# One core: a recurrent-memory attention and a GEGLU layer; shared weight pieces read back from a scratch, the remaining keys loaded by another engine, a copy moved to ACT

## The chip, the core and the metric

The kernel runs on one core of a Trainium2 chip. The metric is the device time of one execution in microseconds. Before the change it is 2309.16 us, the median of three runs (2306.65 to 2320.56).

## What is computed

The input `x` has 2048 rows of 1024. It goes through two layers, and a gate of each row mixes the results:

```python
g = sigmoid((x * gate_w).sum(-1, keepdims=True))
out = g * A(x) + (1 - g) * B(x)

def A(x):                       # 64 segments of 32 rows, one after the other
    mem = mem0                  # 8 rows
    for s in range(64):
        h = concat(mem, x[32*s : 32*s+32])          # 40 rows
        q, k, v = h @ Wq, h @ Wk, h @ Wv            # 32 heads of 128
        p = softmax(mask(q @ k.T * scale))          # memory rows are seen by all
        o = (p @ v) @ Wo
        mem, out_s = o[:8], o[8:]                   # the next segment needs mem

def B(x): return (gelu(x @ w_gate) * (x @ w_up)) @ w_down
```

Only `mem` passes from one segment to the next. Each of Wq, Wk, Wv and Wo has 8 MB, so that A needs 32 MB of weights in every segment.

## The kernel before

**Rows.** Of a segment's 32 rows of `x`, 24 go with the 8 memory rows into `hT`, a block of 32 columns that TensorE (PE) projects in the segment itself. The other 8 rows (the "rest" rows) depend on no memory. They are projected ahead, for four segments at a time, by extra runs of eight products ("fills", lines 839 to 850) that are put between the segment's own. `FILL` (line 883) says which one or two of six fills a segment holds: two for `s % 4` of 0 (k, then q) and 1 (v, then q), one for 2 (v) and 3 (k). Their q and k go to a buffer in HBM, `qk_scr`, and come back a segment at a time into the tile `qkr` (`load_qk`, line 540, 64 KB). `put_rest` (line 879) copies the 8 rest keys of every head out of `qkr` into columns 32 to 39 of `kT`, on GpSimd (POOL). The scores (line 703) read `kT`.

**Halves.** A segment does the heads in two halves, first `ua = s % 2`, then `ub = 1 - s % 2`. In the lists of steps r is 0 for the first half and 1 for the second. The order of a segment's products is written out: k, q and v of the first half (with the end of the last segment's output product between them), then k, q, the first half's output product, v, and the beginning of the second half's output product. `plan(s)` hangs everything else (evacuations, transposes, loads, stores) on points of this list: `on("o", 1, 0, f)` runs f just before piece 0 of the second output product. Each engine works its own instructions in this order.

**Weights.** A weight is cut into pieces of 128 x 2048 (512 KB, 4 KB in each partition), named (matrix, half, i), 64 pieces in all. 36 pieces have an SBUF slot of their own. The other 28 share 14 slots in pairs: pieces k 0 and 1, q 0 and 1, v 0 to 4, o 0, 1, 4, 5 and 6, of both halves. As the order of halves alternates, every shared slot is loaded once in each segment, 14 x 512 KB = 7.3 MB. `spent` (line 455) issues such a load on SyncE's (SP's) queue as soon as PE has used a slot. Neighbouring slots are loaded by one transfer when all of a group are spent; `GROUPS` (line 408) has k 0-1, q 0-1, v 0-1, v 2-3 and o 4-6.

Pieces of q, k and v come from the inputs, in rows of 4 KB. Wo's layout has rows of 1 KB, so in segments 1 to 10 `keep` (line 383) stores the ten shared o pieces into a scratch in HBM, one in a segment, at the point `("k", 0, 4)`. Later loads of o 4-6 come from `wg_scr` in rows of 12 KB, those of o 0 and o 1 from `wo_scr`, one by one, in rows of 4 KB.

**From one segment to the next.** The output product leaves two halves of its sum in different partitions of a PSUM bank. `fold(s, b)` (line 821) copies one of them to the tile `part` and adds the other to it (line 825), both on VectorE (DVE). `next_mem` (line 829) transposes the result on PE and puts the memory columns into the next `hT`.

**Waits.** A small planner (class `_Prog`) finds for every operation the earlier ones that wrote or read the same bytes, or used the same PSUM bank, and makes it wait for those of other engines. Tiles overlay each other: the stage tile `kS` (k before its transpose) and `pAB` (the probabilities) lie on `kT`; stage tiles `0S` and `1S` overlap `oRc`, which the store `o_scr<-oRc` (line 985) reads.

The 64 segments end at 1658 us. Then come the rest rows' output product and, from 1721 us on, the B layer's products, with their own weights; the change touches neither.

Of the kernel before, what the change touches and what calls it, by code (L numbers as in the profile page):

```python
# [210 lines left out]
def bass_gated_mix__memory_aug_recurrent_mem_tr__geglu_ffn__prompt_kernel(  # L211
# [34 lines left out]
    with ExitStack() as es:  # L246
# [16 lines left out]
        a_scr = nc.dram_tensor("a_scr", [NSEG, 4, SEG, 256], BF16)  # L263
        wo_scr = nc.dram_tensor("wo_scr", [16, 128, 2048], BF16)
        wg_scr = nc.dram_tensor("wg_scr", [2, 128, 3, 2048], BF16)

# [104 lines left out]
        def dst(t, k):  # L371
            return t[:, :].rearrange("p (h f) -> p h f", h=4) if k[0] == "o" else t[:, :]

        kept = set()
        wo_at = lambda k: wg_scr[k[1], :, k[2] - 4, :] if 4 <= k[2] < 4 + 3 else wo_scr[8 * k[1] + k[2]]

        def load_piece(t, k, lane):
            if k in kept:
                op("sp", lambda e: e.dma_start(t[:, :], wo_at(k)), rd=[("D", "wo", k)], wr=[t.r()], lane=lane)
            else:  # L380
                op("sp", lambda e: e.dma_start(dst(t, k), src(k)), wr=[t.r()], lane=lane)

        def keep(k):
            t = slots[home[k]]
            op("sp", lambda e: e.dma_start(wo_at(k), t[:, :]), rd=[t.r()], wr=[("D", "wo", k)], lane="wo")
            kept.add(k)
# [20 lines left out]

        GROUPS = {("k", 0): 2, ("q", 0): 2, ("v", 0): 2, ("v", 2): 2, ("o", 4): 3}
        lead = {(m, i + x): (m, i) for (m, i), n in GROUPS.items() for x in range(n)}
        for (m, i), n in GROUPS.items():  # L410
            assert all(home[m, 0, i + x] == home[m, 0, i] + x for x in range(n))
        held = {}
# [7 lines left out]
        def load_group(k0, n):  # L420
            m, u, i = k0
            h = home[k0]
            t, x = (wall, h - nkqv) if m == "o" else (sl, h)
            reg = ("S", slots[h].off, slots[h].off + n * PIECE)
            if m == "o":
                op("sp", lambda e: e.dma_start(t[:, x:x + n, :], wg_scr[u]), rd=[("D", "wo", (m, u, i + y)) for y in range(n)],
                   wr=[reg], lane=f"sl{h}")
            else:
                W = {"q": A_Wq, "k": A_Wk, "v": A_Wv}[m]
                v = W[i * 128:(i + n) * 128, 16 * u:16 * u + 16, :].rearrange("(y p) h e -> p y (h e)", y=n)  # L430
                op("sp", lambda e: e.dma_start(t[:, x:x + n, :], v), wr=[reg], lane=f"sl{h}")
# [243 lines left out]
        def turn(st, bank=TT):  # L675
            def f(e):
                for j in range(4):
                    ins = e.transpose(PBV[bank][:, j * 128:(j + 1) * 128], st[:, j * 128:(j + 1) * 128], ident[:, :])  # L678
                return ins
            op("pe", f, rd=[st.r(), ident.r()], wr=[BK(bank)])  # L680

        def trans(to, st, bank=TT):
            turn(stage[st], bank)
# [5 lines left out]
        b8 = lambda v, n: v.unsqueeze(2).to_broadcast([128, 8, n])  # L689

        def mask():
# [4 lines left out]
        def scores(u, masked=True):  # L696
# [3 lines left out]
            def f(e):  # L700
# [8 lines left out]
                return ins  # L709
            op("pe", f, rd=[qT.r(), qkr.r(256 * u, 256 * u + 128), kT.r()], wr=[BK(SS)])  # L710
            op("pool", lambda e: e.memset(pAB[:, 256:544].bitcast(FP32), 0.0), wr=[pAB.r(256)])
# [13 lines left out]
            def halves(k, w, after):  # L725
                return [op("dve", lambda e, c=c: e.transpose(tAB[:, c + 32 * k:c + 32 * k + 4 * w].rearrange("p (j x) -> p j x", j=4)[:, :, 0:32],  # L726
                                                             pAB[:, c:c + 256].rearrange("p (j k x) -> p j k x", j=4, k=2)[:, :, k, :]),
                           rd=[pAB.r(c, c + 256)], wr=[tAB.r(c, c + 256)], after=[x]) for c, x in zip((0, 256), after)]
            halves(0, 64, halves(1, 56, [fin, fin]))

# [90 lines left out]
        def fold(s, b):  # L821
            lo, hi = slice(64 * b, 64 * b + 64), slice(64 - 64 * b, 128 - 64 * b)
            pt, cs = part, slice(256 * b, 256 * b + 256)
            op("dve", lambda e: e.tensor_copy(pt[lo, :], PB[XO][hi, cs]), rd=[BK(XO)], wr=[pt.r()])  # L824
            return op("dve", lambda e: e.tensor_tensor(out=a_bf[lo, :], in0=PB[XO][lo, cs], in1=pt[lo, :], op=ALU.add),
               rd=[BK(XO), pt.r()], wr=[a_bf.r()])
# [51 lines left out]
        def put_rest():  # L878
            op("pool", lambda e: e.tensor_copy(kT[:, :, :, 32:40].rearrange("p j g c -> p (j g) c"),  # L879
                                               qkr[:, 1, :].rearrange("p (x c) -> p x c", c=8)),  # L880
               rd=[qkr.r(128, 256)], wr=[kT.r()])

# [11 lines left out]
        def fill0(m, r, b, st, G=0, h=hR):  # L894
            run(fill(m, r, b, h))
            fill_evac(m, r, G, b, st)
            fill_put(m, r, G, st)

        def plan(s):
# [8 lines left out]
            def on(m, r, n, *fs, s=s):  # L908
                at.setdefault((s, m, r, n), []).extend(fs)
# [19 lines left out]
            if not last and s == 0:  # L929
                on("k", 0, 4, lambda: load_h(s + 1))  # L930
            if 1 <= s <= 2 * len(PAIRS["o"]):
                on("k", 0, 4, lambda: keep(("o", s % 2, PAIRS["o"][(s - 1) // 2])))
# [243 lines left out]
```

## Time and profile before

| | us |
|---|---|
| median of three runs | 2309.16 |
| the profiled execution, whole | 2311.71 |
| its span, first to last instruction | 2309.9 |
| PE busy in the span | 2069.2 (90%) |
| DVE / ACT / POOL busy | 1044.2 / 541.9 / 423.4 |
| moved by DMA | 638.04 MB, of it 596.58 MB on SP's queue |
| granted PE clock, mean | 0.98 |

The profile page has a map of the span in 40 equal slices of 57.7 us. In it a digit is the busy share in tenths, for each engine and for the 16 DMA engines together. The view of waits names, for an engine, the instruction that waited, what ended the wait, the total, how often, and the longest. The view of windows gives the busy time of the engines in a stretch, and at the end of each row the granted PE clock, the busy share of the DMA engines and the GB/s. The timeline lists instructions with start, duration, engine, line, operation and tiles; a "q" behind an engine's name means that its sequencer issues a transfer. The trace also has a record of every DMA packet: queue, start, duration and size.

### The profile page before, as it was taken

Reading aid. Unit: us, or ns where it says so; the run is one execution under the profiler, and the core shown is the slowest. Engines: PE = TensorE matmul, PEld = TensorE weight load, DVE = VectorE, ACT = ScalarE, POOL = GpSimd, SP = SyncE. Lnnn points to the kernel's source line nnn. Section 1 sums busy time; section 2 is a strip of 40 time slices with the busy share of each in tenths; the row PEclk is TensorE's granted clock in tenths of the full one; section 3 lists DMA queues with packets and bytes.
Section 4 is the critical chain, followed back from the end, with each engine's and each line's share of the span. In section 5 each row is a group of like instructions: output and inputs, shape, how many; then the busy total and the mean of one; then the engine's idle time right before and its main releaser. Section 6 shows DMA issues by size and latency. Waiting matters only on the chain.

```text
span 2309.9 us, 69920 instructions
## 1 busy us (share of the span) xinstructions
PE 2069.2 (90%) x31393; PEld 982.4 (43%) x31393; DVE 1044.2 (45%) x2697; ACT 541.9 (23%) x1111; POOL 423.4 (18%) x819
## 2 busy tenths in 40 slices
PE   4588888989999899898998989988799999999999
PEld 2243443444444444444444444443464444444444
DVE  3344444454444544445444444454315446163462
ACT  1122222222222222222222222221113123032130
POOL 4422212222222221222222222221100000000000
PEclk9699999999999999999999999998999999999999
DMA  9989999999999999999999989998964440803520
GB/s 370 358 299 336 327 337 347 324 341 334 330 346 328 347 322 327 344 318 352 322 340 339 331 313 328 324 344 313 331 214 139 153 148 10 291 19 128 167 88 19
DMA packets 237563, 638.04 MB, mean 276 GB/s; under 512 B 22441, under 2 KB 91305, under 8 KB 230481
## 3 DMA queue, kind: packets, MB, share of 16 engines
q1 hardware_dynamic: 213440, 596.58, 72.9%
q0 software_dynamic: 13888, 26.31, 3.5%
q10 hardware_dynamic: 9936, 10.69, 1.3%
q8 instruction: 247, 4.05, 0.7%
q14 instruction: 52, 0.42, 0.1%
HBM read 596.85 MB, written 36.63 MB: 274 GB/s over the span
## 4 chain that ended last, share of the span: by engine, by line
PE 56%; DMA 32%; DVE 5%; issue 3%; ACT 2%; POOL 1%; SPq 0%; ACTq 0%; POOLq 0%; DVEq 0%
PE pb L780 18%; PE pb L1077 15%; DMA sl<-in_A_Wv_dram 10%; DMA wall<-wg_scr 7%; PE pb L1131 5%; DMA qkr<-qk_scr 3%; PE pb L813 3%; DMA o_scr<-oRc 3%; PE pb L796 3%; PE pb L678 3%; PE pb L850 3%; PE pb L1027 2%; PE pb L1112 2%; DMA sl<-in_A_Wq_dram 1%; DMA xr_scr<-xr 1%
## 5 line engine op out<-in xcount | busy, mean ns | idle before, releaser
L780 PE MATMUL pb<-sl,hT 128*32 128x512 bf16 x12288 | 776.1, 385 | 36.6 <-DMA sl<-in_A_Wv_dram 17.3
L780 PEld LDWEIGHTS pb<-sl,hT 128*32 128x32 bf16 x12288 | 312.5, 97 | 361.4 <-DMA sl<-in_A_Wv_dram 39.8
L850 PE MATMUL pb<-sl,hR 128*32 128x512 bf16 x3072 | 220.7, 392 | 3.5 <-issue 2.9
L1077 PE MATMUL pb<-xT,wg 128*128 128x512 bf16 x896 | 211.7, 379 | 0.8
L1077 PE MATMUL pb<-xT,wu 128*128 128x512 bf16 x896 | 211.7, 379 | 0.0
L813 PE MATMUL pb<-wall,oT 128*32 128x256 bf16 x4056 | 154.1, 278 | 33.7 <-DMA wall<-wg_scr 10.5
L824 DVE COPY part<-pb 64x256 f32<-64x256 f32 x128 | 54.0, 422 | 256.8 <-PE pb L813 256.0
L661 ACT ACTIVATE kS<-pb 128x512 bf16<-128x512 f32 x127 | 75.8, 597 | 385.1 <-PE pb L780 363.7
L796 PE MATMUL pb<-wall,oT 128*32 128x512 bf16 x2048 | 150.4, 389 | 9.8 <-issue 2.9
L763 POOL COPY oRc<-oT 128x128 bf16<-128x128 bf16 x128 | 96.3, 752 | 339.9 <-DVE oT L664 336.8
L1131 PE MATMUL pb<-wd,GT 128*128 128x512 bf16 x672 | 146.6, 379 | 2.7 <-DMA wd<-in_B_w_down_dram 2.6
L1085 ACT ACTIVATE s<-pb 128x512 f32<-128x512 f32 x112 | 66.8, 596 | 313.4 <-PE pb L1077 313.4
L813 PEld LDWEIGHTS pb<-wall,oT 128*32 128x32 bf16 x4056 | 96.9, 97 | 95.8 <-ACT oT L661 25.8
L714 ACT ACTIVATE E<-pb 128x320 bf16<-128x320 f32 x128 | 56.0, 437 | 333.8 <-DVE pb L713 333.8
L1086 DVE SCALAR_TENSOR_TENSOR tp<-s,pb 128x512 f32<-128x512 f32 x112 | 76.9, 687 | 125.9 <-ACT s L1085 125.7
L1077 PEld LDWEIGHTS pb<-xT,wg 128*128 128x128 bf16 x896 | 87.2, 98 | 107.9 <-DVE GT L1093 3.7
L1077 PEld LDWEIGHTS pb<-xT,wu 128*128 128x128 bf16 x896 | 87.7, 98 | 105.7
L879 POOL COPY kT<-qkr 128x128 bf16<-128x128 bf16 x128 | 37.3, 291 | 491.0 <-DVE kT L664 229.4
L664 DVE COPY kT<-pb 128x512 bf16<-128x512 bf16 x128 | 54.4, 425 | 160.9 <-PE pb L678 160.9
L664 DVE CAST oT<-pb 128x160 bf16<-128x160 f32 x256 | 76.5, 320 | 104.4 <-PE pb L746 104.4
L726 DVE STREAM_TRANSPOSE tAB<-pAB 128x128 bf16<-128x128 bf16 x512 | 114.0, 280 | 4.4
L1090 DVE SCALAR_TENSOR_TENSOR tp<-tp,pb 128x512 f32<-128x512 f32 x112 | 77.0, 687 | 78.5 <-ACT tp L1089 78.5
(103 smaller groups left out, 2158.6 us busy)
## 6 DMA issues: line engine op xcount, KB each, us to landing
sl<-in_A_Wv_dram SPq DMA_DIRECT2D x128, 1024.0 KB, 11.2
wall<-wg_scr SPq DMA_DIRECT2D x53, 1536.0 KB, 9.5
sl<-in_A_Wk_dram SPq DMA_DIRECT2D x64, 1024.0 KB, 6.1
sl<-in_A_Wq_dram SPq DMA_DIRECT2D x64, 1024.0 KB, 9.0
wall<-wo_scr SPq DMA_DIRECT2D x120, 512.0 KB, 6.2
wd<-in_B_w_down_dram SPq DMA_DIRECT2D x42, 1024.0 KB, 5.5
sl<-in_A_Wv_dram SPq DMA_DIRECT2D x75, 512.0 KB, 11.4
wall<-in_A_Wo_dram SPq DMA_DIRECT2D x41, 512.0 KB, 7.9
```

The costliest lines, as they stand in the source:

```text
L661: op("act", lambda e: e.activation(o, i, ACTF.Copy), rd=rd, wr=wr)
L664: op("dve", lambda e: e.tensor_copy(o, i), rd=rd, wr=wr, after=after)
L726: return [op("dve", lambda e, c=c: e.transpose(tAB[:, c + 32 * k:c + 32 * k + 4 * w].rearrange("p (j x) -> p j x", j=4)[:, :, 0:32], pAB[: ...
L763: op("pool", lambda e: e.tensor_copy(oRc[:, :, 16 * u:16 * u + 16].rearrange("p c x -> p x c"), oT[:, :, :, 32:40].rearrange("p g j c -> p ...
L780: ins = e.matmul(PB[bk][32 * g:32 * g + 32, :], lhsT=h[:, i, :], rhs=w[:, g * 512:(g + 1) * 512], start=(n == 0), stop=(n == 7))
L796: ins = e.matmul(PB[XO][32 * g:32 * g + 32, :], lhsT=oT[:, j, x, 0:32], rhs=wall[:, na:nb + 1:nb - na, c:c + 256], start=(n == 0 and hp == 0),
L813: ins = e.matmul(PB[XO][32 * g:32 * g + 32, 256 * b:256 * b + 256], lhsT=oT[:, j, x, 0:32], rhs=w[:, c:c + 256], start=False, stop=(n % 4 ...
L850: ins = e.matmul(PB[b][32 * g:32 * g + 32, :], lhsT=h[:, k[2], :], rhs=w[:, g * 512:(g + 1) * 512], start=(n == 0), stop=(n == 7))
L1077: ins = e.matmul(PB[bk][:, 0:FB], lhsT=w[:, kc, cc:cc + 128], rhs=xT[:, :, :, kc, :].rearrange("p t i c -> p (t i) c"), start=(kc == 0), s ...
L1086: op("dve", lambda e, hg=hg, t=t: e.scalar_tensor_tensor(out=t[:, :], in0=s1[:, :], scalar=1.0, in1=hg, op0=ALU.add, op1=ALU.mult), rd=[BK ...
L1090: op("dve", lambda e, hu=hu, t=t: e.scalar_tensor_tensor(out=t[:, :], in0=t[:, :], scalar=1.0, in1=hu, op0=ALU.add, op1=ALU.mult), rd=[BK( ...
L1131: ins = e.matmul(PB[bank[2 * k + hf]][:, :], lhsT=GT[:, j, tb * 128:(tb + 1) * 128], rhs=w[:, jj, hf * 512:(hf + 1) * 512], start=(j == 0) ...
```

## The change

There are four edits.

1. `put_rest` no longer counts as a writer of the whole `kT`. It writes a name of its own, `("K", "rest")`, which the scores read, and waits for the last readers of what lies on `kT` (the PE transposes of k and q, or the DVE transposes of `pAB`), collected in `turned`. The second `put_rest` of a segment is put ahead of the transposition of k.
2. The second load of rest queries and keys of a segment, `load_qk(s, 1)`, is issued by ACT instead of POOL.
3. The groups are now k 0-1, q 0-1, v 0-2, v 3-4, o 0-1 and o 4-6. Every group has a scratch in HBM with the pieces of a row side by side, so rows of 8 or 12 KB. The 18 shared pieces of v, k and q are stored into it in segments 3 to 20, one in each, in this order, at the point `("o", 1, 0)`. A group's transfer reads the scratch as soon as all its pieces are there, and the input before.
4. The first copy of the first `fold` of a segment is on ACT where `s % 4` is 0 or 3.

```diff
+        GROUPS = {("k", 0): 2, ("q", 0): 2, ("v", 0): 3, ("v", 3): 2, ("o", 0): 2, ("o", 4): 3}
+        run_scr = {g: nc.dram_tensor(f"{g[0]}{g[1]}_scr", [2, 128, n, 2048], BF16) for g, n in GROUPS.items()}
-        wo_at = lambda k: wg_scr[k[1], :, k[2] - 4, :] if 4 <= k[2] < 4 + 3 else wo_scr[8 * k[1] + k[2]]
+        def at_scr(k):
+            g = lead[k[0], k[2]]
+            return run_scr[g][k[1], :, k[2] - g[1], :]
...
-        GROUPS = {("k", 0): 2, ("q", 0): 2, ("v", 0): 2, ("v", 2): 2, ("o", 4): 3}
...
-            if m == "o":
-                op("sp", lambda e: e.dma_start(t[:, x:x + n, :], wg_scr[u]), rd=[("D", "wo", (m, u, i + y)) for y in range(n)],
-                   wr=[reg], lane=f"sl{h}")
+            ks = [(m, u, i + y) for y in range(n)]
+            if all(k in kept for k in ks):
+                op("sp", lambda e: e.dma_start(t[:, x:x + n, :], run_scr[m, i][u]), rd=[("D", "w", k) for k in ks], wr=[reg], lane=f"sl{h}")
...
-            op("pe", f, rd=[qT.r(), qkr.r(256 * u, 256 * u + 128), kT.r()], wr=[BK(SS)])
+            op("pe", f, rd=[qT.r(), qkr.r(256 * u, 256 * u + 128), kT.r(), ("K", "rest")], wr=[BK(SS)])
...
-            halves(0, 64, halves(1, 56, [fin, fin]))
+            turned[:] = halves(0, 64, halves(1, 56, [fin, fin]))
...
-            op("dve", lambda e: e.tensor_copy(pt[lo, :], PB[XO][hi, cs]), rd=[BK(XO)], wr=[pt.r()])
+            if b == 0 and s % 4 in (0, 3):
+                act_copy(pt[lo, :], PB[XO][hi, cs], [BK(XO)], [pt.r()])
+            else:
+                dve_copy(pt[lo, :], PB[XO][hi, cs], [BK(XO)], [pt.r()])
...
-               rd=[qkr.r(128, 256)], wr=[kT.r()])
+               rd=[qkr.r(128, 256)], wr=[("K", "rest")], after=turned)
...
+        STORE = [(m, i) for m in "vkq" for i in PAIRS[m]]
...
+            if 3 <= s < 3 + 2 * len(STORE):
+                on("o", 1, 0, lambda: keep((STORE[(s - 3) // 2][0], ub, STORE[(s - 3) // 2][1])))
...
-                on("v", 0, 5, lambda: load_qk(s, 1))
+                on("v", 0, 5, lambda: load_qk(s, 1, "act"))
...
+                on("o", 0, 0, lambda: put_rest())
                 on("o", 0, 0, lambda: trans(kT, ub, A0))
...
-                on("o", 0, 0, lambda: put_rest())
```

More of the change, by code (lines that the diff above doesn't have):

```diff
@@ L263, in bass_gated_mix__memory_aug_recurrent_mem_tr__geglu_ffn__prompt_kernel @@
         a_scr = nc.dram_tensor("a_scr", [NSEG, 4, SEG, 256], BF16)
-        wo_scr = nc.dram_tensor("wo_scr", [16, 128, 2048], BF16)
-        wg_scr = nc.dram_tensor("wg_scr", [2, 128, 3, 2048], BF16)
         PB = [es.enter_context(nc.psum_tensor(f"pb{i}", [128, 512], FP32)) for i in range(8)]
@@ L372, in dst @@
             return t[:, :].rearrange("p (h f) -> p h f", h=4) if k[0] == "o" else t[:, :]
+        GROUPS = {("k", 0): 2, ("q", 0): 2, ("v", 0): 3, ("v", 3): 2, ("o", 0): 2, ("o", 4): 3}
+        lead = {(m, i + x): (m, i) for (m, i), n in GROUPS.items() for x in range(n)}
+        for (m, i), n in GROUPS.items():
+            assert all(home[m, 0, i + x] == home[m, 0, i] + x for x in range(n))
+        run_scr = {g: nc.dram_tensor(f"{g[0]}{g[1]}_scr", [2, 128, n, 2048], BF16) for g, n in GROUPS.items()}
         kept = set()
-        wo_at = lambda k: wg_scr[k[1], :, k[2] - 4, :] if 4 <= k[2] < 4 + 3 else wo_scr[8 * k[1] + k[2]]
+        def at_scr(k):
+            g = lead[k[0], k[2]]
+            return run_scr[g][k[1], :, k[2] - g[1], :]
         def load_piece(t, k, lane):
             if k in kept:
-                op("sp", lambda e: e.dma_start(t[:, :], wo_at(k)), rd=[("D", "wo", k)], wr=[t.r()], lane=lane)
+                op("sp", lambda e: e.dma_start(t[:, :], at_scr(k)), rd=[("D", "w", k)], wr=[t.r()], lane=lane)
             else:
@@ L384, in keep @@
             t = slots[home[k]]
-            op("sp", lambda e: e.dma_start(wo_at(k), t[:, :]), rd=[t.r()], wr=[("D", "wo", k)], lane="wo")
+            op("sp", lambda e: e.dma_start(at_scr(k), t[:, :]), rd=[t.r()], wr=[("D", "w", k)], lane="wo")
             kept.add(k)
@@ L406, in first @@
                 fetch(n)
-        GROUPS = {("k", 0): 2, ("q", 0): 2, ("v", 0): 2, ("v", 2): 2, ("o", 4): 3}
-        lead = {(m, i + x): (m, i) for (m, i), n in GROUPS.items() for x in range(n)}
-        for (m, i), n in GROUPS.items():
-            assert all(home[m, 0, i + x] == home[m, 0, i] + x for x in range(n))
         held = {}
@@ L679, in f @@
                 return ins
-            op("pe", f, rd=[st.r(), ident.r()], wr=[BK(bank)])
+            return op("pe", f, rd=[st.r(), ident.r()], wr=[BK(bank)])
         def trans(to, st, bank=TT):
-            turn(stage[st], bank)
+            turned.append(turn(stage[st], bank))
             dve_copy(to[:, :, :, 0:32].rearrange("p j g c -> p (j g) c"),
@@ L689, in bass_gated_mix__memory_aug_recurrent_mem_tr__geglu_ffn__prompt_kernel @@
         b8 = lambda v, n: v.unsqueeze(2).to_broadcast([128, 8, n])
+        turned = []
         def mask():
```

## The prediction

> **What bounds the kernel now.** The page first: the profiled execution took 2311.71 us, 1.8 us more than its span, and 2.55 us more than the median of the runs. I sum against the profiled execution and take 2.5 off at the end.
>
> ```profile
> span 2309.9 us, 69920 instructions
> ...
> PE   4588888989999899898998989988799999999999
> ...
> DMA  9989999999999999999999989998964440803520
> ...
> q1 hardware_dynamic: 213440, 596.58, 72.9%
> ```
>
> In slices 3 to 28, the segments, PE and the DMA engines are both near full. Which one is late is told by PE's waits in 626 to 1585 us, the 40 segments in which all new groups are in use:
>
> ```profile
> PE pb L834 <- DVE a_bf L825: 21.9, 26, 1.1
> PE pb L703 <- POOL kT L879: 9.7, 11, 3.2
> PE pb L813 <- DMA wall<-wg_scr: 8.9, 13, 1.4
> PE pb L780 <- DMA sl<-in_A_Wv_dram: 6.0, 13, 0.7
> PE pb L813 <- DMA wall<-wo_scr: 5.5, 10, 1.2
> PE pb L780 <- DMA sl<-in_A_Wq_dram: 4.0, 4, 1.7
> ```
>
> Weights cost 24.4 us in 40 waits, rest keys 9.7 us. The view counts from a matmul's modelled end and so too little: at 1026.22 it tells 0.70 us, but the starts are 1.08 us apart, where groups of four follow in 0.21. With 0.17 us more for each wait the weights cost 31 us, 0.8 us of a segment's 24. The fold's 21.9 us is a chain DVE, PE, DVE.
>
> SP's queue and some windows show why weights are late although the engines rest in every segment:
>
> ```profile
> 998.38 0.32 SPq L426 DMA_DIRECT2D wall<-wg_scr  x1
> 998.74 1.38 SPq L540 DMA_DIRECT2D qkr<-qk_scr  x1
> 1005.16 0.32 SPq L985 DMA_DIRECT2D o_scr<-oRc  x1
> 1008.41 0.38 SPq L431 DMA_DIRECT2D sl<-in_A_Wk_dram  x1
> 1009.27 0.70 SPq L431 DMA_DIRECT2D sl<-in_A_Wq_dram  x1
> 1011.47 1.08 SPq L431 DMA_DIRECT2D sl<-in_A_Wv_dram  x2
> 1014.69 0.34 SPq L381 DMA_DIRECT2D sl<-in_A_Wv_dram  x1
> ```
>
> ```profile
> 1005.00:1009.50 4.50, 4.27 (x90) 2.31 (x92) 1.44 (x4) 0.10 (x1) 1.16 (x3) 1.00 0.47 153
> 1009.60:1013.20 3.60, 3.60 (x74) 1.68 (x66) 1.45 (x4) 0.43 (x2) 1.30 (x2) 1.00 0.95 274
> 1020.00:1022.50 2.50, 2.40 (x60) 1.14 (x61) 1.44 (x5) 0.99 (x3) 0.50 (x2) 1.00 1.03 416
> ```
>
> The last but one number is the DMA engines' busy share. A segment's stream starts with k, when PE has used its slots, and ends with o 4-6 some 24 us later, as long as the segment. Between streams lies a lull: in 1005.0 to 1009.5 a share of 0.47, so 4.5 x 0.53 = 2.4 us of all engines. So a shorter stream takes waits away, and a transfer added in the lull may be free.
>
> **Scratch rows.** In the packet records a 4096-byte packet takes 159 ns (median; mean 183), an 8192-byte one 309 (another queue), a 12288-byte one 460 (mean 486). Clean times save 2 x 159 - 309 = 9 ns on 8 KB and 3 x 159 - 460 = 17 on 12 KB. A group of two has 128 packets of 8 KB, 8 on each engine: k, q, v 3-4 and o 0-1 save 4 x 8 x 9 = 0.29 us, v 0-2 saves 8 x 17 = 0.14, together 0.43 us a segment: the low end. By means v 0-2 saves 8 x (3 x 183 - 486) = 0.5 us; k's megabyte takes 3.57 us of engine time, q's 2.97, a later v group's 2.59, and if all pairs came down to 8 x (309 + 26) = 2.68 us, the stream would save 1.6 us: the high end. I take 1.2, nearer to the second, since means are what the stream lives on. Against a mean loss of 0.8 us this takes most waits away: four fifths of 31, **-25 us**. In 342 to 626 us (segments 9 to 20, v in use by stages) weights cost 7.4 us in 9 waits; half of it with the same correction, **-4**.
>
> **Grouping.** PE uses v 3 just before v 4; now both land with v 4, which is the late one, and o 0 with o 1. One more group of four matmuls (0.21 us) waits until the stream has become faster, some ten segments: **+2**.
>
> **Eighteen stores.** The ten stores of o stand in the middle of the stream. The two last, where one o piece at most comes from Wo, had segments of 25.60 and 25.35 us (from one fold's transpose to the next), the next 23.49 and 23.81: 1.5 us or more each, so at most 27 us for 18. The new stores are issued behind o 4-6 and run into the lull: nothing at the low end. But three things queue behind. SP's load of rest keys is needed 5 us later, so is covered. `o_scr<-oRc` lands later, and ACT's evacuation to 0S or 1S waits for it (54.2 and 48.3 us of waits, 4.0 and 1.0 us of them on PE). And the next k group overwrites the slot being stored: its issue at 1008.41, and all SP work behind it, must await a store that cannot end before o 4-6, landed at 1008.77. That holds in four segments for k and in four for q. I take 0.4 us for the ten v stores and 1 us for the eight others: **+12** (0 to 27).
>
> **Rest keys.**
>
> ```profile
> 1014.84 0.29 POOL L879 COPY kT<-qkr 128x128 bf16<-128x128 bf16 x1 [1.76 <-DVE kT L664]
> 1015.43 0.55 POOL L540 DMA_DIRECT2D qkr<-qk_scr  x1 [0.29 <-POOL kT L879]
> 1021.62 0.29 POOL L879 COPY kT<-qkr 128x128 bf16<-128x128 bf16 x1 [5.37 <-DMA qkr<-qk_scr]
> ```
>
> The first copy no longer waits for DVE's copy of kT (0.42 us and its hop), and ACT, free until the exponential 2.4 us later, issues without the 0.29 us that POOL loses: the load starts some 0.75 us earlier. Behind the waiting ACT stand only that exponential and its followers. But POOL's 64 KB go as 16 packets of 4 KB, one an engine (landing 6.0 us after issue), ACT's as 128 of 512 bytes, eight an engine. The nearest rows of ACT's queue under load are the x stores of the beginning: issued at 62.82, first packet at 66.0, last at 68.0, landed at 68.85. There 512-byte packets and SP's alternate (half microseconds from 62.5: 18, 41, 38 against 40, 44, 46). Eight turns beside 8 or 12 KB are 8 x (27 + 309) to 8 x (27 + 486) ns, 2.7 to 4.1 us; with 3.2 before and 0.9 behind 6.8 to 8.2, so the landing is up to 1.4 us later than today. If ACT's start were SP's of an idle stream (1.2 us) it would be 2 us earlier. Today's waits are 12.7 us from 342 on. I take half of them gone, **-6** (-13 to +50).
>
> The Trainium skill ("DMA: Bandwidth & Descriptors", section on queues, rings and completion order) says that an engine drains a whole packet of some 9 to 17 descriptors from one ring before it switches. The alternating counts above do not agree with it; what it would give is the fourth rival.
>
> **Fold.** In segments with s % 4 of 0 and 3 DVE's copy starts 161 ns after the product, else 48: the fill's copy is ahead of it. ACT takes 303 ns for 160 columns and 437 for 320, so some 384 for 256 against 426. 32 x 0.13 = 4 us at best, half of it on the path: **-2**. At worst the extra hop (about 0.05 us) costs +2.
>
> **Sum:** -25 - 4 + 2 + 12 - 6 - 2 = -23, so 2288.7 for the profiled execution and **2286** for the median. One per cent, 23 us, is about what a measurement of this kernel can tell from no change.
>
> **Rivals.**
> - *The rows bring little* (0.25): only the clean 0.43 us, so half of the 31 and nothing before (-15), stores at 20, the rest as above: -15 + 2 + 20 - 3 - 2 = +2, 2311. For it: the late part of the stream already runs at 416 GB/s, and 12 KB rows at about the same. Against it: the 274 GB/s of its beginning.
> - *All waits go and the stores hide* (0.13): -31 - 9 - 13 - 4 = -57, 2252. For it: 2.4 us of lull against 1.5 us a store.
> - *The rest keys become the late transfer* (0.13): eight small packets queue between 12 KB ones, and PE stands before the scores. At the full 1.4 us, in some 40 segments, +50 in place of -6: +33, 2340. It ends slower than before from about 0.6 us a segment. For it: today the copy follows the landing within 0.12 us in most segments, so there is no slack. Against it: the earlier issue.
> - *The rest keys pass in one turn* (0.05): eight rows of 27 ns are 0.2 us, the landing comes 3.2 + 0.2 + 0.9 = 4.3 us after an issue that is 0.75 us earlier, and all 12.7 us go: -30, 2279. Against it: the counts.
>
> **How the numbers follow.** The forecast has 0.44, and runs from 2265 to 2302 by its own terms; two thirds of it lie over 1% faster. Faster by over 1%: 0.29 + 0.13 + 0.05 and a little of the first rival, 0.48. Slower by over 1%: 0.13 and its worst stores, 0.14. The range 2254 to 2325 leaves out the third rival and the tip of the second.
>
> **What would show it.** Right: the weights' waits on PE fall from 24.4 us to a few; k's transfer, landing 6.1 us after issue, lands in about 5; segments from 21 on take 23.2 us instead of 24; POOL's wait for rest keys shrinks. Wrong: the new transfers take as long as before; the wait before L703 grows; SP stands before the k group in segments 14 to 20.

## The result, and the profile after

The changed kernel takes 2345.34 us in the median of four runs (2343.91 to 2354.52), beside 2309.16 for the kernel before, which a fourth run leaves as it is. The ratio is 1.0168, with a 95% interval of 1.0143 to 1.0193: 1.7% longer, clear of the spread of the runs, if short of 2%. The forecast was 2286 in a range of 2254 to 2325; what came is 5 us from the third rival, 2340, "the rest keys become the late transfer".

Lines are numbered anew. The projections are at L784 (L780 before), the output products at L817 and L800 (L813, L796), the scores at L707 (L703), the fold's transpose at L841 (L834), the transposition of q and k at L680 (L678), `put_rest` at L886 (L879), `load_qk` at L542 (L540). Loads from a scratch are issued at L429, from the inputs at L433, stores of pieces at L391. The profile cannot tell a scratch's name apart in `wall<-o_scr`: it stands for o 0-1 as well as o 4-6. The page of the changed kernel, the same rows as before:

```profile
span 2344.2 us, 69748 instructions
...
PE   3588888878889898898989889898799999999999
...
DMA  9999999989988888898898888988865350713520
...
q1 hardware_dynamic: 174384, 606.02, 70.6%
```

The weights' larger rows did what rows can do: SP's queue moves 9.4 MB more (596.58 MB before, and the stores are in it) in 39,000 packets fewer, and its share of engine time falls from 72.9% to 70.6%. In 626 to 1585 us the DMA engines' share falls from 0.93 to 0.88, and PE's row has lost nines as well: both rest more. So the time was not lost to the stream's length. The waits of PE in 626 to 1585 us, the window of the prediction, say where it went:

```profile
PE pb L707 <- POOL kT L886: 56.3, 39, 2.1
PE pb L841 <- DVE a_bf L832: 19.2, 20, 1.0
PE pb L784 <- DVE hT L844: 5.3, 20, 0.3
PE pb L680 <- ACT 0S L663: 5.2, 3, 2.0
PE pb L817 <- DMA wall<-o_scr: 2.2, 4, 1.0
PE pb L680 <- ACT 1S L663: 2.1, 5, 0.7
```

Weights cost 2.2 us where they cost 24.4. The scores' wait for rest keys has risen from 9.7 us in 11 waits to 56.3 in 39, one in nearly every segment. The timeline of POOL and ACT in a segment, the same one (36) whose rows the prediction showed of before:

```profile
1046.25 0.30 POOL L886 COPY kT<-qkr 128x128 bf16<-128x128 bf16 x1 [1.27 <-PE pb L680]
1046.58 0.35 ACTq L542 DMA_DIRECT2D qkr<-qk_scr  x1
1055.29 0.29 POOL L886 COPY kT<-qkr 128x128 bf16<-128x128 bf16 x1 [7.17 <-DMA qkr<-qk_scr]
```

The first copy waits for PE's transpose and no longer for DVE, and the issue follows it after 0.03 us, as forecast. But the second copy now starts 8.71 us after the issue; before it was 6.19 (1015.43 to 1021.62). The transfers by their queue in the window 650 to 1600 us (kind, count, KB, median us from issue to landing):

```profile
sl<-k_scr SPq DMA_DIRECT2D x40, 1024.0 KB, 5.2
sl<-q_scr SPq DMA_DIRECT2D x39, 1024.0 KB, 7.7
qkr<-qk_scr ACTq DMA_DIRECT2D x39, 64.0 KB, 8.5
```

Before, in the same window:

```profile
sl<-in_A_Wk_dram SPq DMA_DIRECT2D x39, 1024.0 KB, 6.1
qkr<-qk_scr POOLq DMA_DIRECT2D x40, 64.0 KB, 6.2
```

and q landed 9.1 us after issue. So the big transfers became faster by 0.9 and 1.4 us and the small one slower by 2.3. The chain that ended last is now led by it, with nearly a fifth of the span:

```profile
DMA qkr<-qk_scr 18%; PE pb L784 16%; PE pb L1088 14%; PE pb L1142 5%; PE pb L817 4%; DMA o_scr<-oRc 3%; PE pb L857 3%; PE pb L1038 2%; PE pb L800 2%; DMA wall<-o_scr 2%; DMA sl<-in_A_Wv_dram 2%; PE pb L1123 2%; PE pb L680 2%; POOL kT L886 1%; DMA xr_scr<-xr 1%
```

**Early and steady.** Taking the start of the first fold's copy into `hT` as the beginning of a segment, folds 0 to 20 cover the segments in which pieces are stored, folds 20 to 60 the 40 segments after. In the profiled executions (2311.71 and 2346.1 us) the early part takes 496.5 us before and 525.9 after, the steady part 963.1 and 971.4. So 29 of the 34 us were lost *early*, where the wait for rest keys is small (13.9 us, before 4.0). The rest keys explain the steady part only. These two parts are given for every kernel below. They are of one execution each: kernels that run the same instructions in the steady part differ there by up to 14 us, so the verdicts rest on the medians and ratios, and the parts only say where.

### The profile page after: what moved, and what is told of

Read it like the earlier page. It is cut to its first block, busy times and chain, and to the rows that moved or that the text cites. A ratio compares the mean times of both kernels' runs of the same rounds, so it can differ in the third digit from the quotient of the medians.

```text
span 2344.2 us, 69748 instructions
## 1 busy us (share of the span) xinstructions
PE 2064.8 (88%) x31368; PEld 997.1 (43%) x31393; DVE 1031.0 (44%) x2665; ACT 554.0 (24%) x1143; POOL 389.7 (17%) x756
## 3 DMA queue, kind: packets, MB, share of 16 engines
q1 hardware_dynamic: 174384, 606.02, 70.6%
## 4 chain that ended last, share of the span: by engine, by line
PE 55%; DMA 33%; DVE 4%; ACT 3%; issue 2%; POOL 2%; ACTq 0%; POOLq 0%; SPq 0%
DMA qkr<-qk_scr 18%; PE pb L784 16%; PE pb L1088 14%; PE pb L1142 5%; PE pb L817 4%; DMA o_scr<-oRc 3%; PE pb L857 3%; PE pb L1038 2%; PE pb L800 2%; DMA wall<-o_scr 2%; DMA sl<-in_A_Wv_dram 2%; PE pb L1123 2%; PE pb L680 2%; POOL kT L886 1%; DMA xr_scr<-xr 1%
## 5 line engine op out<-in xcount | busy, mean ns | idle before, releaser
L784 PE MATMUL pb<-sl,hT 128*32 128x512 bf16 x12288 | 772.9, 387 | 25.8 <-DVE hT L844 8.8
L784 PEld LDWEIGHTS pb<-sl,hT 128*32 128x32 bf16 x12288 | 316.2, 98 | 336.6 <-issue 32.7
L817 PE MATMUL pb<-wall,oT 128*32 128x256 bf16 x4056 | 148.8, 278 | 19.9 <-DMA wall<-o_scr 7.5
L800 PE MATMUL pb<-wall,oT 128*32 128x512 bf16 x2048 | 150.5, 392 | 5.8
L666 DVE COPY part<-pb 64x256 f32<-64x256 f32 x96 | 40.4, 421 | 227.6 <-PE pb L817 227.6
L817 PEld LDWEIGHTS pb<-wall,oT 128*32 128x32 bf16 x4056 | 99.1, 98 | 74.1 <-ACT oT L663 26.7
L886 POOL COPY kT<-qkr 128x128 bf16<-128x128 bf16 x128 | 37.6, 294 | 549.2 <-DMA qkr<-qk_scr 398.6
L716 DVE TENSOR_REDUCE st<-pb 128x8 f32<-128x320 f32 x128 | 62.9, 492 | 135.0 <-PE pb L710 135.0
```

What stands on the lines that cost most here:

```text
L666: op("dve", lambda e: e.tensor_copy(o, i), rd=rd, wr=wr, after=after)
L784: ins = e.matmul(PB[bk][32 * g:32 * g + 32, :], lhsT=h[:, i, :], rhs=w[:, g * 512:(g + 1) * 512], start=(n == 0), stop=(n == 7))
L800: ins = e.matmul(PB[XO][32 * g:32 * g + 32, :], lhsT=oT[:, j, x, 0:32], rhs=wall[:, na:nb + 1:nb - na, c:c + 256], start=(n == 0 and hp == 0),
L817: ins = e.matmul(PB[XO][32 * g:32 * g + 32, 256 * b:256 * b + 256], lhsT=oT[:, j, x, 0:32], rhs=w[:, c:c + 256], start=False, stop=(n % 4 ...
```

## The experiments

All compute the whole result; two of them (3 and 9) store pieces that nothing reads afterwards. The ratio is to the kernel before on the same chip, with its 95% interval.

The medians of the table come from chips on which the kernel before took 2306 to 2309 us; so a difference between two kernels is told as that of their ratios, times 2309 us.

| | kernel | us | ratio | early | steady |
|---|---|---|---|---|---|
| | before | 2309.16 | 1 | 496.5 | 963.1 |
| | the changed kernel | 2345.34 | 1.0168 (1.0143 to 1.0193) | 525.9 | 971.4 |
| 1 | POOL loads the rest keys | 2320.12 | 1.0050 (1.0028 to 1.0071) | 531.7 | 940.6 |
| 2 | 1, no stores of v, k, q | 2330.88 | 1.0089 (1.0055 to 1.0123) | 499.0 | 986.2 |
| 3 | 1, stores made, not read | 2355.93 | 1.0203 (1.0185 to 1.0222) | 530.8 | 972.4 |
| 4 | 2, ACT loads the rest keys | 2323.49 | 1.0062 (1.0045 to 1.0079) | 501.4 | 977.6 |
| 5 | 1, o 0 and o 1 singly | 2289.49 | 0.9932 (0.9908 to 0.9955) | 507.8 | 939.9 |
| 6 | edits 1 and 4 alone | 2302.26 | 0.9982 (0.9970 to 0.9994) | 500.9 | 957.6 |
| 7 | 6, v 0-2 and v 3-4 | 2278.47 | 0.9890 (0.9865 to 0.9914) | 491.2 | 937.8 |
| 8 | 5, pieces stored after `o_scr` | 2282.45 | 0.9906 (0.9875 to 0.9938) | 504.5 | 926.7 |
| 9 | 8, stores made, not read | 2295.12 | 0.9955 (0.9930 to 0.9980) | 508.3 | 936.3 |
| 10 | 5, ACT loads the rest keys | 2340.57 | 1.0152 (1.0117 to 1.0187) | 517.6 | 971.5 |
| 11 | 7, v 0-1 and v 2-4 | 2311.10 | 1.0013 (0.9994 to 1.0031) | 498.7 | 959.3 |
| 12 | 7, ACT loads the rest keys | 2287.40 | 0.9901 (0.9860 to 0.9941) | 491.9 | 948.7 |

**Waits and the granted clock.** One more thing differs between the kernels. The trace records the granted PE clock, and it has stretches of 3.4 us, sometimes two or three on end, at half clock. In them four of PE's products take 427 ns instead of 216, so half of PE's busy time there is lost. In the segments of the 14 profiles such stretches begin 143 times, and each time PE had been busy for 59% or less of the 3.4 us just before, where its mean is 84 to 92%; not every such low stretch is followed by one. This fits with waits that come close together being paid a second time, as lost clock; no run varies that alone. The steady part of a profile is PE's idle time, this loss, and a rest that is nearly the same in every kernel, 850 to 861 us:

| steady part, us | whole | PE idle | lost at half clock |
|---|---|---|---|
| before | 963.1 | 94.5 | 7.3 |
| the changed kernel | 971.4 | 110.5 | 11.0 |
| 1 | 940.6 | 77.3 | 9.8 |
| 2 | 986.2 | 104.3 | 25.7 |
| 3 | 972.4 | 96.8 | 19.8 |
| 6 | 957.6 | 86.8 | 9.6 |
| 7 | 937.8 | 79.0 | 1.5 |

### 1. The rest keys loaded by POOL again

```diff
-                on("v", 0, 5, lambda: load_qk(s, 1, "act"))
+                on("v", 0, 5, lambda: load_qk(s, 1))
```

> The changed kernel, but POOL issues the second load of rest keys again. Theory A (ACT's queue makes the rest keys late, because eight 512-byte packets an engine take turns with 8 and 12 KB ones): the load lands about 6 us after issue instead of 8.4, PE's wait before the scores (line 707) falls from 56.3 us to under 15 in the steady part, and the time to about 2290 us (2280 to 2305). Theory B (with a shorter stream of weights PE waits for the fold and the transposes anyway, and the wait only moves): the wait before the scores falls, others grow, and the time stays above 2325 us.

27 us come back, all of them in the steady part (971.4 to 940.6 us), and all of them waiting: PE idles 33 us less, and the loss at half clock hardly differs. PE's waits in 640 to 1585 us of this kernel:

```profile
PE pb L841 <- DVE a_bf L832: 19.2, 20, 1.0
PE pb L817 <- DMA wall<-o_scr: 19.2, 25, 1.8
PE pb L707 <- POOL kT L886: 3.8, 7, 1.2
```

The load lands 6.2 us after issue, as before the change, and the wait before the scores falls from 56.3 us to 3.8. A part of the gain turns into a new wait: with rest keys in time, PE now stands 19.2 us before o pieces, 1.5 in this window of the changed kernel. So the third rival's mechanism is there, and theory A has the landing and the wait right. Its time, 2280 to 2305 us, did not come: the kernel is still 0.5% slower than before. Steady segments are 0.56 us shorter, the early part is 35 us longer.

### 2, 3 and 4. Without the stores; with stores that nothing reads; ACT's load without them

In 2 the 18 stores of v, k and q are gone, so their loads come from the inputs in rows of 4 KB; the new groups stay. In 3 the stores are made and the loads still come from the inputs. 4 is 2 with the changed kernel's load on ACT.

```diff
 (2, 4)
-            if 3 <= s < 3 + 2 * len(STORE):
+            if False:
 (3)
-            if all(k in kept for k in ks):
+            if m == "o" and all(k in kept for k in ks):
```

> As the kernel with POOL's load, and v, k and q are neither stored nor read from a scratch: they come from the inputs in 4 KB rows, in the new groups. Theory A (rows of 8 and 12 KB take about 25 us of weight waits away, the eighteen stores cost 15 to 25): weight waits come back to some 25 us in the steady part, segments 3 to 20 are shorter by 15 to 25 us than with the stores, and the time is 2295 to 2310 us, near that of the kernel before. Theory B (the stores hide in the lull and cost under 5 us): the time is 20 us or more above that of the kernel with POOL's load.

> As the kernel without stores, but the eighteen stores of v, k and q are made, and never read. The difference to the kernel without them is the price of the stores alone. Theory A (they delay the store of oRc and the next k and q groups, and fill DMA time that is missing in the stream): 15 to 25 us more. Theory B (they run in the lull): under 5 us more.

> ACT issues the second load of rest keys, and v, k and q come from the inputs in 4 KB rows, without stores. Theory A (the turns with large packets make the load late): eight turns beside 4 KB packets take 8 x (27 + 159) ns = 1.5 us instead of 2.7 to 4.1, the load lands 5.5 to 6.5 us after issue, the wait before the scores is at most that of the kernel before (some 13 us), the time 2295 to 2310 us. Theory B (ACT's queue is slow in itself, whatever the row size): it lands 8 us or more after issue and the time is above 2325 us.

Three prices come out. The **stores** alone cost 26 us (2 to 3), and they lie where they are made: early 499.0 to 530.8 us. PE idles 22 us more there and loses 14 more at half clock, and 4 come back in the rest. The **rows** bring 35 us (3 to 1), all of it steady: 972.4 to 940.6. And 2, which has neither, is 21 us slower than the kernel before, though edits 1 and 4 and the grouping are all that it has over it. That is outside both theories of 2: the first had 2295 to 2310 us, the second 20 us or more above 1, and it is 9 above. PE's waits in 640 to 1585 us of 2 point to o:

```profile
PE pb L817 <- DMA wall<-o_scr: 40.1, 32, 2.9
...
PE pb L784 <- DMA sl<-in_A_Wv_dram: 10.4, 19, 1.1
```

With ACT's load (4) the same kernel is no slower, 1.0062 beside 1.0089 with intervals that overlap. Its load lands after 7.0 us, between the two theories (5.5 to 6.5, and 8 or more), and the time is above the first's 2310. So "ACT issues it" is by itself no loss here; runs 10 and 12 come back to that.

### 5. o 0 and o 1 loaded one by one

```diff
-        GROUPS = {("k", 0): 2, ("q", 0): 2, ("v", 0): 3, ("v", 3): 2, ("o", 0): 2, ("o", 4): 3}
+        GROUPS = {("k", 0): 2, ("q", 0): 2, ("v", 0): 3, ("v", 3): 2, ("o", 0): 1, ("o", 1): 1, ("o", 4): 3}
```

(and POOL's load, as in 1)

> The changed kernel with POOL's load, and o 0 and o 1 are loaded one by one again (rows of 4 KB from a scratch), as in the kernel before. Theory A (the pair waits until PE has used both slots, the shorter stream has run dry by then, and o 0-1 and o 4-6 land late): PE's waits for o pieces in the steady part fall from 19.2 us to under 8, and the time from about 2320 to 2300-2310 us. Theory B (o 0-1 in rows of 8 KB is as good, and the waits come from the whole stream): no difference beyond 5 us.

27 us faster than 1, by nothing but two transfers of 512 KB, in rows of 4 KB, in place of one of 1 MB. SP's queue of 1, then of 5, in one segment:

```profile
1030.20 0.32 SPq L533 DMA_DIRECT2D hT<-xq_scr  x1
1031.94 1.19 SPq L429 DMA_DIRECT2D wall<-o_scr  x2
```

```profile
1024.93 0.32 SPq L533 DMA_DIRECT2D hT<-xq_scr  x1
1025.66 1.95 SPq L429 DMA_DIRECT2D wall<-o_scr  x3
```

A slot comes free when PE has used it. The pair must wait for the second slot, so its issue comes 1.74 us after that of `hT`; alone, o 0 is issued after 0.73 us, and PE reads o 0 first. What that costs depends on the rows of the stream. Of the gain, 24 us lie in the early part (531.7 to 507.8), where most loads still have rows of 4 KB; there PE's waits for o, in 107 to 640 us, are in 1

```profile
PE pb L817 <- DMA wall<-o_scr: 18.0, 13, 2.5
```

and in 5

```profile
PE pb L817 <- DMA wall<-o_scr: 6.8, 9, 1.3
```

In the steady part, with large rows, the waits differ less (19.2 and 13.6 us, where theory A had under 8) and the time hardly (940.6 and 939.9 us). The packet records show why there is room: in the 4 us from the issue of `hT` the DMA engines' mean share is 0.99 before, 0.68 in 1 and 0.82 in 5. The stream has run dry before the o loads are issued, and they land sooner.

### 6, 7 and 11. Which grouping of v

6 is the kernel before with edits 1 and 4 alone: the groups of before, no stores of v, k and q, POOL's load. 7 takes v 0-2 and v 3-4 into it. 11 takes v 0-1 and v 2-4.

```diff
 (6)
+        GROUPS = {("k", 0): 2, ("q", 0): 2, ("v", 0): 2, ("v", 2): 2, ("v", 4): 1, ("o", 0): 1, ("o", 1): 1, ("o", 4): 3}
 (7)
+        GROUPS = {("k", 0): 2, ("q", 0): 2, ("v", 0): 3, ("v", 3): 2, ("o", 0): 1, ("o", 1): 1, ("o", 4): 3}
 (11)
+        GROUPS = {("k", 0): 2, ("q", 0): 2, ("v", 0): 2, ("v", 2): 3, ("o", 0): 1, ("o", 1): 1, ("o", 4): 3}
```

> The kernel before with the new rule for the copy of the rest keys (fewer waits, earlier place) and the first fold copies on ACT; POOL loads the rest keys, groups and rows are the old ones, no store of v, k or q. Theory A (the new groups are what makes the kernel without stores 20 us slower than the kernel before): 2295 to 2310 us, o waits in the steady part near 14 us as before. Theory B (the copy's new place or the fold on ACT costs it): 2320 us or more.

> The kernel with the old groups and no stores, but v in the groups 0-2 and 3-4; o 0 and o 1 stay one by one. Theory A (of the new groups only o 0-1 costs time): within 5 us of the 2302 us of the kernel with the old groups. Theory B (the v groups cost as well, since v 3 now lands with v 4): 2310 us or more, with v waits above 14 us in the steady part.

> The kernel with v 0-2 and v 3-4 in one transfer each, o 0 and o 1 singly, no stores of v, k and q (2278.5 us), here with the groups v 0-1 and v 2-4 instead. Old groups v 0-1, v 2-3, v 4 gave 2302.3. Theory A: what gains is one transfer fewer, 2 instead of 3 for v (the last group is issued by one instruction, no short transfer of 512 KB at its end): then this is as fast, 2274 to 2286. Theory B: what gains is that the first v transfer is issued later (it waits for three slots), so that k and q land first, and the second comes with little: then the first group of two is as early as with the old groups and most of the gain goes, 2290 to 2304. The wait for v at the projections tells it too: 20 us in the steady segments with A, about 14 with B.

Edits 1 and 4 bring 4 us (6): the first theory's time, though o waits are 8.2 us and not 14. v 0-2 with v 3-4 bring 21 more, which neither theory of 7 had (2302, or 2310 and more), and 7 at 2278.47 us is the fastest kernel of all, 1.1% under the kernel before. One transfer fewer is not what does it: 11 has two for v as well and is 28 us slower than 7. So the first theory of 11 falls. Its second, that the gain is the later issue of the first v transfer, has the sign, but 2311.10 us lie past its range, and the wait is another than it expected: PE's waits for v in 640 to 1585 us are 20.0 us in 7, and in 11

```profile
PE pb L784 <- DMA sl<-in_A_Wv_dram: 40.2, 35, 2.4
```

where about 14 was expected. The last v group lands 18.8 to 19.0 us after the segment's start in all three kernels (medians of the steady segments). In 11 it holds v 2, 3 and 4, and PE stands before v 2 with three pieces' products still to do; in 7 v 2 is there at 16.0 us. That fits with 11 being slow. It does not explain why 7 beats 6, where v 2 and 3 land at 17.5 us and only v 4 comes last: the waits for v *rise* from 14.4 us in 6 to 20.0 in 7, those for o fall from 8.2 to 3.7, which adds up to no gain, and still the steady segments are 0.5 us shorter, 20 us in all. The table on the clock has where they are: PE idles 7.8 us less in all and loses 8.1 us less at half clock. Why the waits of 7 come together less often is left open.

The pair o 0-1 can now be priced in another surrounding: 2 is 7 with the pair, and is 46 us slower. The rows of v, k and q have 4 KB to the end in both, and now the steady part has the loss (937.8 to 986.2 us). PE waits 40.1 us for o and 10.4 for v in 2; in 7

```profile
PE pb L784 <- DMA sl<-in_A_Wv_dram: 20.0, 30, 1.7
PE pb L817 <- DMA wall<-o_scr: 3.7, 11, 0.7
```

With 2.6 us for q in 7, the weights' waits are 24 us longer in 2, and PE idles 25 us more. The other half of the 48 us is the clock, as the windows of the steady part say, of 2 and then of 7. Behind the length stands PE's busy time, third from the end the granted clock: the same 17592 products take 23 us more.

```profile
625.97:1612.24 986.27, 881.95 (x17592) 417.27 (x17588) 452.09 (x1378) 250.57 (x558) 238.72 (x487) 0.97 0.91 324
619.22:1556.98 937.76, 858.75 (x17592) 407.76 (x17586) 452.08 (x1379) 250.75 (x558) 239.90 (x487) 1.00 0.95 341
```

Over whole executions the clock was 0.970 to 0.973 in all four of 2 and 0.982 to 0.984 in all four of 7. Singly, o 0 lands 20.2 and o 1 21.5 us after the segment's start, the pair 22.1, and o 4-6 behind it 26.4 where it was 25.4.

### 8 and 9. The pieces stored behind `o_scr<-oRc`; the same, not read

```diff
-            if 3 <= s < 3 + 2 * len(STORE):
-                on("o", 1, 0, lambda: keep((STORE[(s - 3) // 2][0], ub, STORE[(s - 3) // 2][1])))
...
             on("o", 1, 0, lambda: op("sp", lambda e: e.dma_start(o_scr[s], oRc[:, :, :].rearrange("p c x -> p (c x)")),
                                      rd=[oRc.r()], wr=[("D", "o", s)], lane="sto"))
+            if 3 <= s < 3 + 2 * len(STORE):
+                on("o", 1, 0, lambda: keep((STORE[(s - 3) // 2][0], ub, STORE[(s - 3) // 2][1])))
```

> As the kernel with o 0 and o 1 one by one, and the store of a v, k or q piece is issued behind the store of oRc instead of ahead of it. Theory A (the piece's store delays that of oRc, and ACT's evacuations to 0S and 1S, and PE with them, wait for it): the waits on 0S and 1S in segments 3 to 20 fall from about 17 us to under 5 and the time by 10 to 15 us, to about 2290. Theory B (the store costs DMA time wherever it stands): the waits move to the k and q weights, and the time changes by less than 5 us.

> The best kernel so far (POOL's load, o 0 and o 1 one by one, stores behind the store of oRc), but the stored v, k and q are never read. Against the kernel without stores it gives the price of the stores, against the best one the worth of the rows. Theory A: stores 10 to 15 us, rows 30 to 40 us, so 2310 to 2325 us. Theory B (the stores cost their DMA time wherever they stand): 25 us or more for the stores, so 2327 us or more.

8 is 6 us faster than 5, with intervals that overlap, so the gain is not certain; where it is, is plain. The store of `o_scr` in the early window 165 to 590 us, then PE's waits for the stage tiles in 107 to 640 us, of 5:

```profile
o_scr<-oRc SPq DMA_DIRECT2D x17, 64.0 KB, 6.3
```

```profile
PE pb L680 <- ACT 1S L663: 9.9, 5, 3.2
PE pb L680 <- ACT 0S L663: 9.0, 5, 2.2
```

and of 8:

```profile
o_scr<-oRc SPq DMA_DIRECT2D x17, 64.0 KB, 4.4
```

```profile
PE pb L680 <- ACT 1S L663: 3.1, 4, 1.3
PE pb L680 <- ACT 0S L663: 2.3, 5, 0.7
```

Queued behind half a megabyte, the small store lands 1.9 us later; ACT's evacuation to `0S` or `1S` waits for it, and PE for ACT: 18.9 us, 5.4 in the later place. It was 4.2 before the change and 18.3 after. So the wait falls as theory A of 8 had it, and the time by half of what it had.

9 makes the same stores and does not use them. Beside 7 it prices stores in the later place at 15 us; beside 8 it prices the rows at 11 us (the intervals overlap a little), where both theories had 30 to 40. So with o loaded singly the scratch of v, k and q brings 11 us for 15, and 7 without it is no slower than 8.

### 10 and 12. ACT's load where nothing else is late

10 is 5, and 12 is 7, each with the rest keys loaded by ACT. In 10 the stream has rows of 8 and 12 KB except for o 0 and o 1, in 12 rows of 4 KB except for o 4-6.

> The changed kernel with o 0 and o 1 one by one; ACT issues the load of rest keys, as in the change. Theory A (the late rest keys cost what they cost, whatever the o loads do): it lands about 8.5 us after issue, PE's wait before the scores stays at 50 us or more in the steady part, and the time is 20 to 35 us above the kernel with POOL's load (2289). Theory B (the wait before the scores hides behind the o waits and is paid once only): under 10 us above it.

> The same kernel (2278.5 us) with the second load of rest keys issued by ACT instead of POOL; all rows of v, k and q have 4 KB here. Theory A (the load's 512-byte packets wait a turn each, so the cost grows with the size of the packets beside them): it lands about 7 us after issue as it did beside 4 KB rows before, 0.8 us later than POOL's, and costs 5 to 20 us: 2284 to 2298, far from the 51 us that the same edit cost beside rows of 8 and 12 KB. Theory B (what costs is that ACT issues it, whatever lies beside it): 2320 to 2335, and the scores wait for rest keys some 50 us in the steady segments.

The one line costs 51 us in 10, more than either theory had; in 12 it costs 3 by the ratios (9 by the medians), with intervals that overlap. PE's waits in 640 to 1585 us, of 10 and of 12:

```profile
PE pb L707 <- POOL kT L886: 55.7, 38, 2.3
```

```profile
PE pb L707 <- POOL kT L886: 8.8, 15, 1.1
```

and the load's landing in 10 and in 12:

```profile
qkr<-qk_scr ACTq DMA_DIRECT2D x39, 64.0 KB, 8.5
```

```profile
qkr<-qk_scr ACTq DMA_DIRECT2D x40, 64.0 KB, 7.0
```

So what lies beside the load decides, and not by itself who issues it. The packet records say how. ACT's load is recorded as 128 packets of 512 bytes, 27 ns each, eight for each of the 16 DMA engines. From issue to first packet, from first to last, and to the landing it takes 3.41, 4.28 and 0.78 us in the changed kernel, and 3.51, 2.79 and 0.72 in 12. Only the middle part differs: 0.53 us for each of the eight turns beside 8 and 12 KB packets (309 and 460 ns alone), 0.35 beside 4 KB (159 ns). In that time packets of other transfers start, 1.6 for each of ACT's in the changed kernel, of 313 ns in the mean, and 2.0 of 164 ns in 12: 27 + 1.6 x 313 is 0.53 us, 27 + 2.0 x 164 is 0.35. So one of ACT's packets passes for nearly two of the others, and the wait grows with the time that those take.

## Why the prediction was wrong

The kernels of the table make a chain from before to after, in which each differs from the last by one thing:

| from, to | what is added | us | the prediction's term |
|---|---|---|---|
| before, 6 | edits 1 and 4 | -4 | -2 for the fold; edit 1 a part of -6 |
| 6, 7 | v 0-2, v 3-4 | -21 | grouping +2, with the next |
| 7, 2 | o 0-1 | +46 | |
| 2, 3 | the eighteen stores | +26 | +12 |
| 3, 1 | rows of 8 and 12 KB | -35 | -25 - 4 |
| 1, after | ACT loads the rest keys | +27 | -6, with edit 1 |
| | sum | +39 | -23 |

The forecast missed by 62 us: 33 by ACT's load, 23 by the grouping, 14 by the stores, -6 by the rows and -2 by the rest. The chain is one order of the steps, and the prices are not additive: the pair costs 46 us here, 27 beside POOL's load and large rows (1, 5) and 4 beside ACT's (after, 10; the intervals overlap). That two waits of a segment cover each other fits with the waits for `wall<-o_scr`, 19.2 us in 1 and 1.5 in the changed kernel, but is not tested further. ACT's load costs 27 with the pair and 51 without it.

- **The step that failed: the rest keys, "half of them gone, -6".** The prediction had worked out the mechanism itself, eight turns beside 8 or 12 KB and a copy with no slack behind the landing, and gave it a chance of 0.13. But its own bounds left no gain to halve: 6.8 to 8.2 us after an issue that is 0.75 us earlier is 6.05 to 7.45 on today's clock, and the row shown was 6.0. "Half" had no row behind it. The landing came after 8.5 us, above the top of the bounds (the turns took 4.28 us, where at most 4.1 was worked out, as 1.6 other packets pass in a turn and not one), and cost 27 to 51 us, at the upper end of "-13 to +50". The alternating packet counts were the right row to read, and by them and the bounds a later landing was likelier than a gain; the counts are those of the 512-byte store ahead, though, while the store whose start and end it took (62.82 to 68.85) has packets of 2 KB.
- **Grouping, +2**, was mis-sized in both of its halves: the o pair is +27 to +46 with POOL's load, v -21. The prediction counted what PE waits for at the end of a group (one more product of four) and left out the beginning: a group is issued when its *last* slot comes free, so the pair goes out 1 us later than o 0 alone. The prediction had named the issue as the point where a stream begins, and still costed the edit at the end of the group. About half of the 46 us is PE at half clock (24 of 48 us in the steady part); the prediction adds up waits at their own length and has no term for that. This is the largest single price of the chain, and no rival had it.
- **The stores, +12 (0 to 27)**, measured 26 in the chain and 15 in the later place, inside the bounds and twice the value taken. Of the three things that were to queue behind them, the load of rest keys was covered, as it said (PE waits 1.0 us for them in 107 to 640 us of 1). The other two are in the trace: the store of `o_scr` lands later and costs PE some 14 us more in waits for `0S` and `1S`, which was priced at nothing of its own; and SP stands before the k and q groups in four segments each, as forecast, its own waits:

```profile
SPq L143 <- DMA k_scr<-sl: 21.5, 4, 6.4
...
SPq L143 <- DMA q_scr<-sl: 11.0, 4, 3.9
```

- **The rows, -29**, were right in kind and near in size (-35 in the chain, -11 with o single: a part of the 35 is the pair's price given back). k lands 5.2 us after issue, "in about 5" was forecast, and the weights' waits went from 24.4 to 2.2 us. The gain shows in the segment only where nothing else is late, 23.5 us in 1 and 23.2 in 8; with ACT's load it is 24.3. Forecast was 23.2.
- **The fold, -2, and edit 1**: together -4 (interval -7 to -1), near what was forecast. ACT's copy takes 381 ns, 384 was worked out. Its row in the changed kernel:

```profile
L663 ACT ACTIVATE part<-pb x32: 381/381/382, 124.3 to 1695.5; 64x256 f32<-64x256 f32 x32
```

  The copy starts 52 ns after the product, not 161, and takes some 44 ns less, so 0.15 us leaves each of 32 chains, 5 us at best.
- **The signs to look for.** Of those that were to show it right, k's landing and the weights' waits came; POOL's wait for rest keys did not shrink but grew, from 129.1 us in 640 to 1585 to 261.2. Of those that were to show it wrong, the growing wait before the scores and SP standing before the k groups both came.
- **The third rival** gave 2340 (its own terms, +33, make 2342) for 2345.34, and its mechanism is shown (1, 10, 12). Its sum is near by accident all the same: it put the whole loss into forty segments at 50 us, where the chain has 27, and did not have the 29 us of the early part, which come from the stores and the o pair (531.7 us early in 1, where ACT loads nothing; 507.8 without the pair, 499.0 without the stores).

One row of the Trainium skill was weighed in the prediction ("DMA: Bandwidth & Descriptors", section on queues, rings and completion order: an engine drains a whole packet of some 9 to 17 descriptors before it turns to another queue). Runs 10 and 12 speak against it for this load: drained in one turn, its eight rows of an engine would take 8 x 27 ns = 0.2 us from first to last, and the time would not depend on its neighbours; it took 2.8 us beside 4 KB packets and 4.3 beside larger ones. The rival built on that rule, 2279, did not come.

## What to carry to other kernels

A faster stream moves the end to the small transfer beside it: before its rows are made larger, ask which 64 KB load shares the engines, into how many packets its queue cuts it, and how much slack its reader has. A group of loads is issued when its last slot comes free; where the reader stands close behind the loads, a first piece issued early can be worth more than a larger transfer, so compare in the timeline when each slot of the group is spent. Add up PE's waits, but look at the granted clock as well: here waits that came close together went with half clock, and the pair's loss was half of it. And a store that is put into an idle stretch of the engines still stands ahead of every later transfer of its queue: put it behind the small one that something waits for.

## What the runs showed of the hardware

- The same 64 KB load is 16 packets of 4 KB on POOL's queue and 128 of 512 bytes on ACT's, and the two behave differently under load. ACT's first packet comes 3.4 us after issue, POOL's 0.36 to 0.89 (before, 1, 7); between two of ACT's packets nearly two of the others pass (1.6 to 2.0), so its landing went from 7.0 to 8.5 us with the neighbours' packet size, while POOL's was 6.2 beside large rows (1) and 5.6 to 6.3 beside 4 KB (3, 7, 6, before).
- Larger packets moved more with less engine time (72.9% to 70.6% for 9.4 MB more), but the total of a kernel whose scratch had to be written first did not gain by them: ratios of 0.9906 with it (8) and 0.9890 without (7), with intervals that overlap.
- The o pair, worth 27 to 46 us with rest keys in time, cost 4 us beside late ones, with intervals that overlap. Prices of waits do not add up.
- Every one of 143 half-clock periods in the segments stands behind 3.4 us in which PE was busy for 59% or less, and takes 3.4 us or two or three times that; four products take 427 ns in it instead of 216. In 2 they cost 25.7 us of the 40 steady segments, in 7 1.5.
